# Loading k and q of the first eight attention units with consecutive rows per partition, and transposing them head by head as matmuls

## The chip, the cores and the metric

The kernel runs on one core of one Trainium2 chip. The metric is the device time of one execution in microseconds (us), and the median of three executions is compared. The engines are called as in the profile: PE (TensorE, with PEld for its weight loads), DVE (VectorE), ACT (ScalarE), POOL (GpSimd) and SP (SyncE, which issues nearly all DMA transfers; SPq is its queue).

## The reference

Attention over q, k and v of shape [4 batches, 8 heads, 576 positions, 64], then two feed-forward stages. The attention is the sum of a coarse part (q, k and v averaged over groups of four positions, a softmax over 144 keys, the result repeated four times) and a local part (each query sees the keys at a distance below 4).

```
q_d, k_d, v_d = (t.reshape(B, H, Sd, 4, D).mean(axis=3) for t in (q, k, v))
out_up = np.repeat(sm_attn(q_d, k_d, v_d), 4, axis=2)
mask = np.abs(pos[:, None] - pos[None, :]) < 4
scores = np.where(mask, scale * np.matmul(q, k.transpose(0, 1, 3, 2)), -1e9)
out_local = np.matmul(softmax(scores), v)
x = (out_up + out_local) as [2304 tokens, 512]
x = (silu(x @ w_gate) * (x @ w_val)) @ w_out              # 512 -> 1536 -> 512
h = x @ w_in
y = (np.maximum(h, 0) + alpha * np.minimum(h, 0)) @ w2_out # 512 -> 2048 -> 512
```

The weights arrive as float64, so their transfers are twice as large as float32 ones, and each is taken apart on the chip into a high and a low float32r part.

## The kernel before, in words

The attention is cut into 32 units. Unit n is two heads (hp = n mod 4) of one half of 288 queries of one batch; units 0 to 3 are the first half of batch 0 and load all of k (576 rows) and q, units 4 to 7 are its second half and load q alone, since they reuse k of units 0 to 3. These eight (NPRO = 8) run ahead of the feed-forward work, in buffers that weights will take later; units 8 to 31 are strewn into the first feed-forward stage and load k and q in another way (lines 198 to 209), which the change leaves alone.

In a unit, a_load (line 194) issues the transfers of k and q, a_T (line 288) transposes both through PSUM and copies them into kT and qT, with one column for each position, and sums groups of four columns into kd and qd; a_QK makes the local scores in 24 small matmuls per head and the coarse ones in one, and reads columns of qT and kT in the order of positions; a_EXP and a_NRM are the softmax; a_vd sums v over groups of four (line 344, DVE); a_PT and a_PV transpose the coarse weights, multiply with v and write the result as xh and xl, the inputs of the feed-forward stage.

The transfers all go through SP in an order written out by hand in the key `lo='asvtwb01x23'`: a is k and q of units 0 to 3, s and t copy v into overlapping windows in DRAM (line 260 and 266), v loads v for the sums (line 227), w loads the windows back for units 0 to 3 (line 249), b is q of units 4 to 7, the digits are the weights of feed-forward columns j = 0 to 3 (lines 104 and 106), and x loads the windows of units 4 to 7. Each k load takes one head: `k[b, h0 + h].rearrange("(r p) c -> p r c", p=QB)`, so partition p (of QB = 96) gets rows p, p + 96, p + 192 and so on, each a run of 64 floats or 256 bytes in DRAM. q is loaded in the same way, 3 rows per partition. A transpose of such a block of 96 rows and two heads (128 columns) yields 96 consecutive positions, so that the copies out of PSUM (lines 310 to 312 and 319) write consecutive columns.

The splitting of weights is prep1 and w_split (lines 509 and 124): ACT lines 129, 137 and 142, DVE line 139, and POOL or DVE line 143. A planner lays out the order of the instructions of each engine by a simulated timeline; `tc.issue_after` holds the weight work of j = 0 and 1 behind the softmax of unit 3 (gates, key 8), and the sums of line 344 behind the scores of unit 3 on DVE (line 719). From the first matmul of line 488 on, PE works through 96 feed-forward blocks of stage one and then stage two.

Of the kernel before, what the change touches and what calls it, by code (L numbers as in the profile page):

```python
# [23 lines left out]
def attn_moe_moe2_kernel(  # L24
# [13 lines left out]
    nc = tc.nc  # L38
    B, H, S, D = q.shape
# [129 lines left out]
    def at_(n, shape, tag):  # L169
        return wp.tile(shape, F32, tag=pslot[tag, n], name=tag)  # L170
# [23 lines left out]
    def a_load(n):  # L194
        b, half, hp, blk = coords(n)
        h0, t0 = 2 * hp, half * HB
        d = hu[n] = {}
        if n >= NPRO:

            loads = [("qn", q, HB, t0)]  # L200
            if half == 0:
                loads.insert(0, ("kn", k, S, 0))
            for tag, src, rn, r0 in loads:
                t = d[tag] = ap_.tile([128, rn], F32, tag=tag, name=tag, bufs=1)
                for i in range(4):
                    nc.sync.dma_start(
                        out=t[32 * i:32 * (i + 1)].rearrange("r (m c) -> r m c", c=32),
                        in_=src[b, h0 + i // 2, r0:r0 + rn, 32 * (i % 2):32 * (i % 2 + 1)].rearrange("(m r) c -> r m c", r=32))
            return
        if half == 0:  # L210
            kn = d["kn"] = at_(n, [QB, 6, 2, D], "kn")
            for h in range(2):
                nc.sync.dma_start(out=kn[:, :, h], in_=k[b, h0 + h].rearrange("(r p) c -> p r c", p=QB))
        t = at_(n, [128, 2 * NW * 2 * D], "qv").rearrange("p (a w h c) -> p a w h c", a=2, w=NW, h=2)
        d["vw"] = t[:, 1]
        qn = d["qn"] = t[:QB, 0]
        for h in range(2):
            nc.sync.dma_start(out=qn[:, :, h], in_=q[b, h0 + h, t0:t0 + HB, :].rearrange("(r p) c -> p r c", p=QB))

    def a_load_v(n):  # L220
        b, half, hp, blk = coords(n)
# [30 lines left out]
    def stage(b, halves=(0, 1)):  # L252
# [32 lines left out]
        else:  # L285
            win(g0, g1)

    def a_T(n, A):
        b, half, hp, blk = coords(n)
        d = hu[n]  # L290
        idn = ident[:QB, :QB]
        small(n)
        qT, qd = d["qT"], d["qd"]
        nc.gpsimd.memset(qT[:, HB:HB + 8], 0.0)  # L294
        if half == 0:
            kT = kTs[hp] = ap_.tile([128, KW], F32, tag=f"kT{hp}", name="kT", bufs=1)
            nc.gpsimd.memset(kT[:, 0:3], 0.0)
            nc.gpsimd.memset(kT[:, S + 3:KW], 0.0)
            kd = kds[hp] = ap_.tile([128, SD], F32, tag=f"kd{hp}", name="kd", bufs=1)
        if n >= NPRO:  # L300
            if half == 0:
                nc.vector.transpose(out=kT[:, 3:S + 3], in_=d["kn"])
            nc.vector.transpose(out=qT[:, 0:HB], in_=d["qn"])
        elif half == 0:
            for r in range(6):
                nc.tensor.transpose(A[:, r // 3, (r % 3) * QB:(r % 3 + 1) * QB], d["kn"][:, r].rearrange("p h c -> p (h c)"), idn)
            for r in range(NW):
                dst = A[:, 1, HB + QB * r:HB + QB * (r + 1)] if r < 2 else A[:, 0, 320:320 + QB]
                nc.tensor.transpose(dst, d["qn"][:, r].rearrange("p h c -> p (h c)"), idn)
            nc.scalar.copy(out=qT[:, 0:2 * QB], in_=A[:, 1, HB:HB + 2 * QB])  # L310
            nc.scalar.copy(out=qT[:, 2 * QB:HB], in_=A[:, 0, 320:320 + QB])
            nc.scalar.copy(out=kT[:, 3:S + 3].rearrange("c (f t) -> c f t", f=2), in_=A[:, :, 0:HB])
        else:
            for r in range(NW):
                nc.tensor.transpose(A[:, 0, QB * r:QB * (r + 1)], d["qn"][:, r].rearrange("p h c -> p (h c)"), idn)
            if K["qtA"]:
                nc.scalar.copy(out=qT[:, 0:HB], in_=A[:, 0, 0:HB])
            else:
                nc.vector.tensor_copy(qT[:, 0:HB], A[:, 0, 0:HB])
        if half == 0:  # L320
            if 0 < n < NP:
                kq = kT[:, 3:S + 3].rearrange("c (g r) -> c g r", r=4)
                k2 = d["sm"][:, :, 0:SD].rearrange("c h g -> c g h")
                nc.gpsimd.tensor_tensor(out=k2, in0=kq[:, :, 0:2], in1=kq[:, :, 2:4], op=ALU.add)
                nc.gpsimd.tensor_tensor(out=kd, in0=k2[:, :, 0], in1=k2[:, :, 1], op=ALU.add)
            else:
                nc.vector.reduce_sum(kd, kT[:, 3:S + 3].rearrange("c (g r) -> c g r", r=4), axis=AX.X)
        if 0 < n < NP:
            kq = qT[:, 0:HB].rearrange("c (g r) -> c g r", r=4)
            k2 = d["sm"][:, 1, 0:2 * QD].rearrange("c (g h) -> c g h", h=2)  # L330
            nc.gpsimd.tensor_tensor(out=k2, in0=kq[:, :, 0:2], in1=kq[:, :, 2:4], op=ALU.add)
            nc.gpsimd.tensor_tensor(out=qd, in0=k2[:, :, 0], in1=k2[:, :, 1], op=ALU.add)
        else:
            nc.vector.reduce_sum(qd, qT[:, 0:HB].rearrange("c (g r) -> c g r", r=4), axis=AX.X)
# [537 lines left out]
```

## Time and profile before

| | before |
|---|---|
| median of 3 runs | 1009.46 us (1009.44 to 1010.22) |
| span of the profiled execution | 1008.6 us |
| busy: PE, DVE, ACT, POOL | 970.5, 479.7, 307.6, 380.0 us |
| DMA packets, bytes | 135888, 77.80 MB |
| of them under 512 bytes | 97401 |
| k loads of units 0 to 3 | 8 of 144 KB |
| q loads of units 0 to 7 | 16 of 72 KB |

The profiled execution's own time is its span, 1008.6 us from the first to the last instruction; the 0.9 us to the median lie around it. PE is busy for 96% of the span, so the parts of the span in which it isn't are what a change outside the matmuls can reach. The page shows them at the start: in the first two of its 40 slices PE is at 5 and 6 tenths, and DMA at 7 to 9 tenths in the first four. Times in the tables are in us from the start of the span; the granted clock is 1.00 at TensorE's full 2.4 GHz and 0.50 at 1.2 GHz.

### The profile page before, as it was taken

How to read it: one execution, taken by the hardware profiler on the slowest of the kernel's cores; microseconds unless marked ns; L12 is line 12 of the kernel's file. 1: busy time of each engine (PE TensorE's matmuls, PEld its weight loads, DVE VectorE, ACT ScalarE, POOL GpSimd, SP SyncE). 2: the span in 40 equal slices, each digit the busy share in tenths (PEclk: the TensorE clock that was granted, in tenths of full speed). 3: DMA queues.
4: the chain of work that ended last, by engine and by line, in shares of the span. 5: the costliest groups of instructions: out<-in, count | busy, mean ns of one | idle time of the engine just before them, and what ended most of it. 6: DMA issues, size and time to landing. Idle time of an engine off the chain costs nothing.

```text
span 1008.6 us, 19231 instructions
## 1 busy us (share of the span) xinstructions
PE 970.5 (96%) x7760; PEld 866.4 (86%) x7760; DVE 479.7 (48%) x1010; ACT 307.6 (30%) x699; POOL 380.0 (38%) x488
## 2 busy tenths in 40 slices
PE   5689899999999999999999999999999999999998
PEld 4488799999999999999999997888888888888897
DVE  5886874464535464545432769623222222322232
ACT  4598632222222222222223656312111111211111
POOL 6487852244322334222223436624223222322222
PEclk9799999999999999999999999999999999999999
DMA  7899731132111221111104883102000100100010
GB/s 185 254 337 340 174 89 35 27 82 56 41 38 33 70 45 41 44 23 21 41 9 141 287 255 106 32 1 79 6 0 21 53 1 1 47 7 0 1 43 21
DMA packets 135888, 77.80 MB, mean 77 GB/s; under 512 B 97401, under 2 KB 127097, under 8 KB 135033
## 3 DMA queue, kind: packets, MB, share of 16 engines
q1 hardware_dynamic: 135735, 76.57, 26.9%
q8 instruction: 60, 0.98, 0.4%
q14 instruction: 29, 0.24, 0.1%
q10 hardware_dynamic: 64, 0.01, 0.0%
HBM read 67.12 MB, written 15.73 MB: 82 GB/s over the span
## 4 chain that ended last, share of the span: by engine, by line
PE 81%; DMA 7%; DVE 4%; SPq 3%; POOL 2%; ACT 2%; issue 1%; POOLq 0%; DVEq 0%; ACTq 0%
PE y L625 7%; PE y L627 7%; PE y L626 7%; PE g L488 6%; PE v L489 6%; PE v L488 6%; PE g L489 6%; PE g L490 6%; PE v L490 5%; PE y L488 4%; PE y L490 4%; PE y L489 4%; PE h L488 3%; PE h L490 3%; PE h L489 3%; DMA raw<-in_moe_w_out_dram 3%
## 5 line engine op out<-in xcount | busy, mean ns | idle before, releaser
L613 POOL TENSOR_TENSOR gl<-t,gh 128x512 fp32r<-128x512 f32 (+1 forms) x80 | 97.1, 1214 | 250.6 <-ACT gh L612 244.3
L612 ACT CAST gh<-t 128x512 fp32r<-128x512 f32 (+1 forms) x80 | 46.1, 578 | 278.5 <-DVE t L609 238.8
L488 PE MATMUL g<-xh,w 128*128 128x288 f32 x384 | 117.7, 306 | 10.4 <-DVE u L528 5.4
L490 PE MATMUL g<-xh,w 128*128 128x288 f32 x384 | 115.0, 300 | 0.8 <-POOL qT L294 0.8
L488 PE MATMUL v<-xh,w 128*128 128x288 f32 x384 | 115.7, 301 | 0.1
L489 PE MATMUL v<-xl,w 128*128 128x288 f32 x384 | 115.1, 300 | 0.0
L489 PE MATMUL g<-xl,w 128*128 128x288 f32 x384 | 114.8, 299 | 0.0
L489 PE MATMUL y<-pl,w 128*128 128x288 f32 x384 | 113.9, 299 | 0.8 <-POOL pl L538 0.8
L625 PE MATMUL y<-w,gh 128*128 128x512 f32 x288 | 113.2, 393 | 1.0 <-ACT sy L557 1.0
L490 PE MATMUL v<-xh,w 128*128 128x288 f32 x384 | 113.3, 295 | 0.0
L490 PE MATMUL y<-ph,w 128*128 128x288 f32 x384 | 113.0, 297 | 0.0
L626 PE MATMUL y<-w,gh 128*128 128x512 f32 x288 | 112.8, 392 | 0.0
L627 PE MATMUL y<-w,gl 128*128 128x512 f32 x288 | 112.0, 392 | 0.0
L528 DVE SCALAR_TENSOR_TENSOR u<-u,g 128x288 f32<-128x288 f32 x96 | 43.3, 451 | 143.0 <-ACT u L527 142.9
L488 PE MATMUL y<-ph,w 128*128 128x288 f32 x384 | 110.9, 302 | 0.0
L538 POOL TENSOR_TENSOR pl<-u,ph 128x288 fp32r<-128x288 f32 x96 | 81.6, 850 | 56.9 <-ACT ph L537 56.5
L143 POOL TENSOR_TENSOR w<-st,w 128x512 fp32r<-128x512 f32 x52 | 70.7, 1366 | 55.6 <-ACT w L142 55.3
L488 PEld LDWEIGHTS g<-xh,w 128*128 128x128 f32 x384 | 73.3, 191 | 14.2 <-DVE u L528 7.4
L607 DVE TENSOR_SCALAR t<-h,alpha 128x512 f32<-128x512 f32 (+1 forms) x40 | 27.9, 696 | 110.7 <-PE h L490 109.5
L488 PEld LDWEIGHTS y<-ph,w 128*128 128x128 f32 x384 | 70.8, 189 | 4.5 <-issue 4.4
L490 PEld LDWEIGHTS g<-xh,w 128*128 128x128 f32 x384 | 73.6, 192 | 1.1 <-POOL qT L294 1.1
L527 ACT ACTIVATE u<-g 128x288 f32<-128x288 f32 x96 | 39.3, 409 | 115.4 <-PE g L490 109.3
(197 smaller groups left out, 2148.2 us busy)
## 6 DMA issues: line engine op xcount, KB each, us to landing
raw<-in_moe_w_out_dram SPq DMA_DIRECT2D x28, 512.0 KB
raw<-in_moe_w_in_dram SPq DMA_DIRECT2D x16, 512.0 KB
raw<-in_moe_w_gate_dram SPq DMA_DIRECT2D x12, 512.0 KB
raw<-in_moe_w_val_dram SPq DMA_DIRECT2D x12, 512.0 KB
vw<-vwin SPq DMA_DIRECT2D x48, 96.0 KB
out_dram<-os SPq DMA_DIRECT2D x18, 256.0 KB
sy<-y SPq DMA_DIRECT2D x16, 256.0 KB
y<-ys SPq DMA_DIRECT2D x14, 288.0 KB
```

The costliest lines, as they stand in the source:

```text
L143: eng.tensor_sub(w[:, 1], st, f32(w[:, 0]))
L488: nc.tensor.matmul(o, lhi, rhi, start=first, stop=False)
L489: nc.tensor.matmul(o, lhi, rlo, start=False, stop=False)
L490: nc.tensor.matmul(o, llo, rhi, start=False, stop=last)
L527: nc.scalar.activation(out=u, in_=GV[0][:, :HB], func=AF.Tanh, scale=0.5)
L528: nc.vector.scalar_tensor_tensor(out=u, in0=u, scalar=1.0, in1=GV[0][:, :HB], op0=ALU.add, op1=ALU.mult)
L538: nc.gpsimd.tensor_sub(pl, u, f32(ph))
L612: nc.scalar.copy(out=gh[:, :n], in_=t[:, :n])
L613: nc.gpsimd.tensor_sub(gl[:, :n], t[:, :n], f32(gh[:, :n]))
L625: nc.tensor.matmul(o, gh[:, ms], ohi, start=(j == 0), stop=False)
L626: nc.tensor.matmul(o, gh[:, ms], olo, start=False, stop=False)
L627: nc.tensor.matmul(o, gl[:, ms], ohi, start=False, stop=(j == F2 - 1))
```

## The change

For units 0 to 7, one transfer loads both heads of k, and one both heads of q. A partition gets consecutive rows: 6 of k per head (a run of 1536 bytes in DRAM) and 3 of q (768 bytes). In SBUF a tile then lies by head, row and channel. Since the two heads of one row are no longer side by side, the new helper two_T makes each transpose from two matmuls with the identity as the moving operand, one per head, into the lower and the upper 64 partitions of PSUM. A transposed block now holds every sixth (k) or every third (q) position, so the copies out of PSUM put the columns back in order: they write with a step of 6 or 3 floats. Everything behind kT and qT is as before.

```diff
@@ -208,14 +208,14 @@
                         in_=src[b, h0 + i // 2, r0:r0 + rn, 32 * (i % 2):32 * (i % 2 + 1)].rearrange("(m r) c -> r m c", r=32))
             return
         if half == 0:
-            kn = d["kn"] = at_(n, [QB, 6, 2, D], "kn")
-            for h in range(2):
-                nc.sync.dma_start(out=kn[:, :, h], in_=k[b, h0 + h].rearrange("(r p) c -> p r c", p=QB))
+            kn = d["kn"] = at_(n, [QB, 2, 6, D], "kn")
+            nc.sync.dma_start(out=kn.rearrange("p h r c -> p h (r c)"),
+                              in_=k[b, h0:h0 + 2].rearrange("h (p r) c -> p h (r c)", p=QB))
         t = at_(n, [128, 2 * NW * 2 * D], "qv").rearrange("p (a w h c) -> p a w h c", a=2, w=NW, h=2)
         d["vw"] = t[:, 1]
-        qn = d["qn"] = t[:QB, 0]
-        for h in range(2):
-            nc.sync.dma_start(out=qn[:, :, h], in_=q[b, h0 + h, t0:t0 + HB, :].rearrange("(r p) c -> p r c", p=QB))
+        qn = d["qn"] = t[:QB, 0].rearrange("p w h c -> p (w h c)").rearrange("p (h r c) -> p h r c", h=2, r=NW)
+        nc.sync.dma_start(out=qn.rearrange("p h r c -> p h (r c)"),
+                          in_=q[b, h0:h0 + 2, t0:t0 + HB, :].rearrange("h (p r) c -> p h (r c)", p=QB))
 
     def a_load_v(n):
         b, half, hp, blk = coords(n)
@@ -285,12 +285,17 @@
         else:
             win(g0, g1)
 
+    def two_T(dst, src, idn):
+        for h in range(2):
+            nc.tensor.matmul(dst[64 * h:64 * h + 64], src[:, h], idn, start=True, stop=True)
+
     def a_T(n, A):
         b, half, hp, blk = coords(n)
         d = hu[n]
         idn = ident[:QB, :QB]
         small(n)
         qT, qd = d["qT"], d["qd"]
+        qR = qT[:, 0:HB].rearrange("c (p r) -> c r p", r=NW)
         nc.gpsimd.memset(qT[:, HB:HB + 8], 0.0)
         if half == 0:
             kT = kTs[hp] = ap_.tile([128, KW], F32, tag=f"kT{hp}", name="kT", bufs=1)
@@ -303,20 +308,21 @@
             nc.vector.transpose(out=qT[:, 0:HB], in_=d["qn"])
         elif half == 0:
             for r in range(6):
-                nc.tensor.transpose(A[:, r // 3, (r % 3) * QB:(r % 3 + 1) * QB], d["kn"][:, r].rearrange("p h c -> p (h c)"), idn)
+                two_T(A[:, r // 3, (r % 3) * QB:(r % 3 + 1) * QB], d["kn"][:, :, r], idn)
             for r in range(NW):
                 dst = A[:, 1, HB + QB * r:HB + QB * (r + 1)] if r < 2 else A[:, 0, 320:320 + QB]
-                nc.tensor.transpose(dst, d["qn"][:, r].rearrange("p h c -> p (h c)"), idn)
-            nc.scalar.copy(out=qT[:, 0:2 * QB], in_=A[:, 1, HB:HB + 2 * QB])
-            nc.scalar.copy(out=qT[:, 2 * QB:HB], in_=A[:, 0, 320:320 + QB])
-            nc.scalar.copy(out=kT[:, 3:S + 3].rearrange("c (f t) -> c f t", f=2), in_=A[:, :, 0:HB])
+                two_T(dst, d["qn"][:, :, r], idn)
+            nc.scalar.copy(out=qR[:, 0:2], in_=A[:, 1, HB:HB + 2 * QB].rearrange("c (r p) -> c r p", r=2))
+            nc.scalar.copy(out=qR[:, 2], in_=A[:, 0, 320:320 + QB])
+            nc.scalar.copy(out=kT[:, 3:S + 3].rearrange("c (p f r) -> c f r p", f=2, r=NW),
+                           in_=A[:, :, 0:HB].rearrange("c f (r p) -> c f r p", r=NW))
         else:
             for r in range(NW):
-                nc.tensor.transpose(A[:, 0, QB * r:QB * (r + 1)], d["qn"][:, r].rearrange("p h c -> p (h c)"), idn)
+                two_T(A[:, 0, QB * r:QB * (r + 1)], d["qn"][:, :, r], idn)
             if K["qtA"]:
-                nc.scalar.copy(out=qT[:, 0:HB], in_=A[:, 0, 0:HB])
+                nc.scalar.copy(out=qR, in_=A[:, 0, 0:HB].rearrange("c (r p) -> c r p", r=NW))
             else:
-                nc.vector.tensor_copy(qT[:, 0:HB], A[:, 0, 0:HB])
+                nc.vector.tensor_copy(qR, A[:, 0, 0:HB].rearrange("c (r p) -> c r p", r=NW))
         if half == 0:
             if 0 < n < NP:
                 kq = kT[:, 3:S + 3].rearrange("c (g r) -> c g r", r=4)
```

## Rows read from the trace of the kernel before

**Rows 1.** Busy time by stage: us, engines (instructions), granted clock, DMA share, GB/s

```profile
0.00:36.00 36.00, 22.06 (x326) 16.77 (x326) 22.76 (x61) 14.58 (x49) 19.34 (x59) 1.00 0.71 183
36.00:59.00 23.00, 13.75 (x232) 11.02 (x232) 19.22 (x46) 21.28 (x52) 16.08 (x21) 0.70 1.04 327
59.00:75.00 16.00, 16.00 (x179) 15.01 (x180) 12.49 (x27) 14.66 (x40) 14.37 (x16) 0.90 0.91 328
75.00:97.00 22.00, 20.83 (x163) 19.39 (x161) 15.17 (x25) 18.25 (x39) 17.27 (x16) 1.00 1.06 372
97.00:135.00 38.00, 32.27 (x313) 29.30 (x314) 33.39 (x64) 23.97 (x48) 30.75 (x32) 0.96 0.68 157
```

**Rows 2.** Chain that ended last, in order of time: start, us, what

```profile
20.08 9.09 DMA qv<-vwin
...
33.66 5.85 DMA raw<-in_moe_w_out_dram
...
58.94 0.61 PE g L488
...
60.27 0.24 PE g L489
...
63.44 0.13 PE v L488
```

**Rows 3.** SP's queue in order of time: start, us, line, transfer, count

```profile
0.74 0.94 SPq L213 DMA_DIRECT2D kn<-in_k_dram  x2
...
8.07 1.03 SPq L218 DMA_DIRECT2D qv<-in_q_dram  x2
...
29.59 2.97 SPq L218 DMA_DIRECT2D qv<-in_q_dram  x6
...
32.60 0.47 SPq L106 DMA_DIRECT2D raw<-in_moe_w_gate_dram  x1
```

**Rows 4.** DMA in steps of 2 us: us, clock, DMA share, GB/s

```profile
4.00:6.00 2.00, 1.00 0.98 215
6.00:8.00 2.00, 1.00 1.05 215
...
36.00:38.00 2.00, 1.00 1.08 385
```

**Rows 5.** PE in order of time: start, us from first start to last end

```profile
6.76 1.19 PE L306 MATMUL y<-ident,kn 96*128 96x96 f32 x6 [0.71 <-DMA kn<-in_k_dram]
...
15.10 0.42 PE L309 MATMUL gv<-ident,qv 96*128 96x96 f32 x1
...
41.73 1.17 PE L465 MATMUL gv<-bd,qv 128*64 128x96 f32 x12
...
43.90 0.74 PE L315 MATMUL y<-ident,qv 96*128 96x96 f32 x3
```

**Rows 6.** POOL in order of time, units 1 to 3

```profile
7.44 1.30 POOL L676 COPY mask<-tmp 32x128 f32<-32x128 f32 x4
...
19.80 0.31 POOL L332 TENSOR_TENSOR qs<-qs 128x72 f32<-128x72 f32 x1
```

**Rows 7.** Who waited for whom up to 40 us: total us, times, longest

```profile
POOL qs L386 <- DVE mx L373: 2.9, 2, 1.8
```

**Rows 8.** DVE in order of time, from the scores of unit 3

```profile
21.83 0.32 DVE L369 TENSOR_TENSOR qs<-gv,mask 128x192 f32<-128x192 f32 x1
...
24.30 7.76 DVE L344 TENSOR_REDUCE vs<-vd 72x128 f32<-72x512 f32 x8
...
37.66 0.69 DVE L139 SCALAR_TENSOR_TENSOR st<-st 128x512 int32<-128x512 int32 x1 [0.76 <-ACT st L137]
```

**Rows 9.** Groups by shape, first 60 us: busy us, mean ns of one

```profile
L344 DVE TENSOR_REDUCE vs<-vd 72x128 f32<-72x512 f32 x8 | 7.8, 1036 | 0.0
...
L370 DVE TENSOR_REDUCE mx<-y 72x2 f32<-72x288 f32 x4 | 1.8, 444 | 0.0
...
L312 ACT COPY kT<-y 128x576 f32<-128x576 f32 x2 | 1.3, 664 | 0.0
```

## The prediction, made before the changed kernel ran

> **What bounds the kernel now.** I read the stages first. Up to 36 us PE is busy for 22.1 of 36 us, and much of that is short matmuls that wait for one another; from 59 to 75 us it is busy throughout; between 97 and 135 us it has 5.7 us of idle time once more [rows 1]. What runs before 59 us is therefore a lead-in that PE cannot shorten, and whatever moves the first lasting feed-forward matmul (line 488 at 58.94 us) moves the end, if the weights behind it move as well.
>
> The chain of waits says what the lead-in is made of: the transfers of the windows, then the first weight (w_out) landing, each as long as 9.09 and 5.85 us, and then ACT, POOL and DVE steps up to the matmul [rows 2]. So I read SP's queue. Units 0 to 3 cost it sixteen issues, from 0.74 us to the end of the last at 9.10 us, a pitch of (9.10 - 0.74) / 16 = 0.52 us; the eight q loads of units 4 to 7 stand before the weights, six of them in 2.97 us, 0.50 us each; the first weight is issued at 32.60 us [rows 3]. DMA is at the limit at the same time: 215 GB/s at a share of 0.98 to 1.05 while the 256-byte runs of k and q are under way, against 385 GB/s at 1.08 when weights with runs of 1 KB and more follow [rows 4].
>
> Last I read the engines. After the mask is copied (end 8.74 us) POOL makes kd and qd of units 1 to 3 up to 20.11 us [rows 6], and in between it waits 2.9 us for DVE, twice [rows 7]. DVE takes up unit 3's scores at 21.83 us, then spends 7.76 us on the sums of v, and is at the first weight (line 139) at 37.66 us, having idled 0.76 us [rows 8]. From 36 to 59 us ACT is busy for 21.3 of 23 us and DVE for 19.2 [rows 1]: there the engines bound the lead-in.
>
> **The transfers of units 0 to 3.** Sixteen issues become eight. I keep 0.52 us for one, since the first weight's issue, of 512 KB, takes 0.47 us [rows 3] and bytes thus hardly count; the ends are 0.47 and 0.94 us (the two it replaces). The stage transfers then start 8 x 0.52 = 4.2 us earlier (at worst 0, at best 4.6). The bytes stay: 4 x (295 + 147) KB = 1.77 MB. At 215 GB/s they take 8.2 us, at 385 GB/s 4.6 us, so DMA gives back 3.6 us. The runs of 768 and 1536 bytes have no row of their own; I take the weights' rate as the nearer, with 215 GB/s (no gain) as the other end. Issue and data agree on about 4 us for unit 3's k and q; unit 0's wait for the first bytes hardly shrinks.
>
> **The transfers of units 4 to 7.** Eight issues become four, 4 x 0.50 = 2.0 us, and 0.59 MB go from 2.7 to 1.5 us. They stand ahead of the weights, so the first weight can be issued up to 4.2 + 2.0 = 6.2 us earlier, near 26.4 us. No wait is added; a transfer of two heads lands as one, so that a unit's first transpose waits for both heads, as it does now, since each block holds both.
>
> **The transposes.** 36 for units 0 to 3 and 12 for units 4 to 7 become 96 matmuls of half the width. Now, six take 1.19 us; taking off the tail of one (about 0.37 us), the pitch is 0.82 / 5 = 0.16 us. The same shape as the new ones exists: line 465 is a plain matmul of 64 stationary and 96 moving columns into alternating halves of PSUM, twelve in 1.17 us, a pitch of (1.17 - 0.37) / 11 = 0.073 us. Line 315's three transposes right after it, in the same low-clock stretch, take 0.74 us, a pitch of 0.18 [rows 5]. A pair thus costs 0.15 where a transpose costs 0.16 to 0.18: nothing, and I count nothing (ends: -0.02 and +0.16 us for a pair, the latter if two halves don't overlap; nine pairs of a unit then cost 1.4 us). In units 0 to 3 the ACT and POOL chains cover them; without that cover they would add the 1.4 us for each of three units.
>
> A page speaks against this. The Trainium skill ("TensorE: Matmul & The Clock Gate", Terms) says that transpose mode is 4x faster for float32; by it the new matmuls would be four times as dear as what they replace. Line 465's rows disagree with it for this shape [rows 5]; it stays as a rival below.
>
> **The copies out of PSUM.** They write with a step of 12 bytes (q) or 24 (k). No row shows a strided write on ACT or DVE. The nearest is a strided read: line 344 reads with a step of 256 bytes and takes 1036 ns for 512 elements; line 370 reads 288 in a row in 444 ns, and at that pace, 1.54 ns each, 512 would take 789 ns [rows 9]. That is 31% more. On line 312 (664 ns [rows 9]) it is 0.2 us, with lines 310 and 311 0.35 us for a unit. I take +0.4 us on the path in all: two DVE copies of line 319 (0.14 us each) stand directly ahead of line 139, and one ACT copy ends the load of unit 3. The bounds are 0 and a doubling, which is 1.2 us for each of units 0 to 3.
>
> The Trainium skill ("SBUF — State Buffer", Door 1) says that an access which crosses to a new 16-byte line each time pays a penalty; k's step of 24 bytes does, q's of 12 mostly does. It gives no figure, so the sum stays by line 344.
>
> **What of it reaches the end.** The 4 us of arrival are not all taken up. Unit 0 is hardly earlier, the mask stays at 8.74 us, and POOL then has 11.37 us up to 20.11, of which it waits 2.9 us [rows 6, 7]. Earlier k and q can remove that wait and little more. I take 2.6 us of the 2.9, since unit 1's k, which PE waits 0.71 us for [rows 5], no longer holds the chain. DVE's scores of unit 3 go from 21.83 to about 19.2 us, and with them the sums of v and all up to line 139. The 0.76 us of idle there is a wait for the first weight, which comes 6 us earlier: it goes. The sum is 2.6 + 0.76 - 0.4 = 3.0 us at line 139. From 36 to 97 us DMA is at a share of 0.91 to 1.06 [rows 1]; the weight stream starts earlier by more than 3 us, so it does not hold this back, and the 5.7 us of later idle hang on the same conversions, moved by the same amount. What is late next is ACT and DVE between 36 and 59 us.
>
> By the profiled execution, a span of 1008.6 becomes 1005.6 us; with the 0.9 us around it, and so beside the median of 1009.46, I predict **1006.5 us**. Its own range, by the bounds of arrival (2.0 to 3.1 us) and of the copies (0 to 1.2 us), is 1005 to 1008 us.
>
> **The rivals.**
> - *More passes.* The planner uses the weights that come 6.2 us earlier to fill the ACT time left before 36 us (14.6 of 36 us busy [rows 1]), so that the crowded stretch behind it thins out as well. The full 6.2 us: 1003.3 us. Against it: the weight work is held behind unit 3's softmax. Chance 0.17.
> - *It is hidden.* ACT and DVE are full from 36 to 59 us; if the work there is what sets line 488, and the planner fills the time in front with nothing, only the 0.76 us go: 1008.7 us. Chance 0.22.
> - *Slower: PE overtakes.* The planner lays out a new order, and PE's blocks come ahead of the conversions they need. The clock falls when PE idles: it is 0.70 from 36 to 59 us, and at half clock a feed-forward matmul takes 0.24 us where it takes 0.13 later [rows 1, 2]. A block of 24 matmuls at half clock costs 24 x 0.11 = 2.6 us. Two such blocks and the gain lost give 1009.5 + 5.2 = 1014.7 us, one gives 1012.1. It decides from the point at which PE's idle time between 97 and 135 us grows by more than the 3.0 us gained. Chance 0.13, about 1012.
> - *The transposes are dear.* At four times the pitch, nine blocks cost 9 x 0.49 = 4.4 us more in a unit, which no longer fits between its copies; 3 units behind one another cost 13 us less 3 us: 1020 us. Chance 0.03.
> - *It doesn't do what it says.* If runs of 768 bytes and more moved no faster than 256, the eight larger transfers would still be bound by 8.2 us of data; what is left is the 2.0 us of issues that stand ahead of the weights and 0.76 us at line 139 at best: 1008.7 to 1009.5 us. Chance 0.05, with the hidden case for sign.
>
> **How the numbers follow.** The forecast has 0.40. A measurement of this kernel can tell about 0.2%, 2.0 us, from no change. Faster by more: the forecast nearly whole (0.38) and the first rival (0.17), with a few of the hidden case, 0.58 in all. Within: the rest of the hidden case, the case of no faster transfer and the edge of the forecast, 0.26. Slower: the two dear cases, 0.16. For 8 in 10 the range runs from 1002.5, which takes in most of the first rival, to 1011.5 us, which leaves out most of those two.
>
> **What would show it.** Right: the k and q loads of units 0 to 3 end on SP's queue near 4.9 us and the first weight is issued near 27 us; the DMA rate in 2 to 6 us is above 300 GB/s; packets fall by about 6900 (9216 of 256 bytes against 768 and 1536); POOL's two waits are shorter; DVE takes up unit 3's scores near 19 us and line 488 begins near 56 us; a pair of new matmuls keeps the pitch of 0.15 us. Wrong: line 488 still near 59 us with the transfers early (hidden); the copies at more than 1.3 times their durations; a granted clock below 0.96 between 97 and 135 us with more idle time there (PE overtakes).

## The result and the profile after

The changed kernel takes 1023.48 us (median of 4 runs, 1022.08 to 1024.77) where the kernel before takes 1009.45: a ratio of 1.0133, 95% interval 1.0120 to 1.0147, or 14.0 us more, where 3 us less was forecast. Its profiled execution took 1024.4 us, with a span of 1022.3 us against 1008.6.

The transfers did what the change says. SP's queue of the kernel after, answering [rows 3] (start, us, line, transfer, count):

```profile
5.18 0.45 SPq L217 DMA_DIRECT2D qv<-in_q_dram  x1
5.67 0.96 SPq L260 DMA_DIRECT2D vwin<-in_v_dram  x1
...
25.32 0.92 SPq L217 DMA_DIRECT2D qv<-in_q_dram  x2
26.30 1.22 SPq L106 DMA_DIRECT2D raw<-in_moe_w_gate_dram  x1
```

Eight issues end at 5.63 us, and the first weight is issued at 26.30 us instead of 32.60. The page's count of packets, against 135888 and 97401 before:

```profile
DMA packets 128785, 77.82 MB, mean 76 GB/s; under 512 B 87993, under 2 KB 119993, under 8 KB 127929
```

The rate rose little. The same 2-us windows as in [rows 4], of after (the last two figures are DMA's share and GB/s):

```profile
4.00:6.00 2.00, 1.70 (x22) 1.73 (x24) 0.00 (x0) 0.00 (x0) 2.00 (x10) 1.00 0.83 213
6.00:8.00 2.00, 2.00 (x29) 2.00 (x28) 0.00 (x0) 0.51 (x3) 1.88 (x13) 1.00 1.10 249
```

PE shows what the transposes became. PE of after in order of time, answering [rows 5]:

```profile
4.30 2.19 PE L290 MATMUL att<-ident,kn 96*64 96x96 f32 x24 [4.30 <-DMA kn<-in_k_dram]
6.25 1.20 PE L290 MATMUL att<-ident,qv 96*64 96x96 f32 x12
...
14.68 0.76 PE L366 MATMUL y<-kT,qs 64*32 64x32 f32 x48
16.47 0.76 PE L370 MATMUL y<-kd,qs 64*72 64x144 f32 x4 [1.03 <-POOL qs L338]
17.16 0.42 PE L290 MATMUL y<-ident,qv 96*64 96x96 f32 x1
```

A k is 12 matmuls, since it has six blocks and a pair for each, yet the row counts 24 records: a plain float32 matmul leaves two records, a transpose one (and so does a feed-forward matmul, in float32r). The local scores show it too: line 366 makes 24 matmuls for a unit, 12 for each of its two heads and not 24, in 48 records. The block takes 2.19 us where six transposes took 1.19 [rows 5], a q takes 1.20 instead of some 0.7. The last rows show an order that before did not have: the last matmul of unit 2's q (17.16) stands behind unit 1's coarse scores (16.47, line 370), which wait 1.03 us for POOL. ACT of after shows the same kind of order, and the copies with a step:

```profile
7.49 0.41 ACT L315 COPY qs<-att 128x192 f32<-128x192 f32 x1 [4.63 <-PE att L290]
7.75 0.29 ACT L316 COPY qs<-att 128x96 f32<-128x96 f32 x1
7.88 1.20 ACT L317 COPY kT<-att 128x576 f32<-128x576 f32 x1
...
16.41 0.72 ACT L433 ACTIVATE qs<-qs,sr 72x144 f32<-72x144 f32 x2 [0.93 <-DVE sr L422]
17.78 0.42 ACT L315 COPY qs<-y 128x192 f32<-128x192 f32 x1 [0.65 <-PE y L290]
```

Line 317 takes 1.20 us where line 312 took 0.66 [rows 9]. Unit 2's copies (17.78) stand behind the softmax scaling of unit 0 (line 433). So the units run one behind another, and DVE gets to unit 3's scores, and to the first weight, later than in [rows 8]. DVE of after:

```profile
29.89 0.36 DVE L375 TENSOR_TENSOR qs<-gv,mask 128x192 f32<-128x192 f32 x1
...
30.98 7.78 DVE L350 TENSOR_REDUCE vs<-vd 72x128 f32<-72x512 f32 x8
...
42.77 0.69 DVE L139 SCALAR_TENSOR_TENSOR st<-st 128x512 int32<-128x512 int32 x1
...
79.44 0.34 DVE L375 TENSOR_TENSOR qs<-att,mask 128x192 f32<-128x192 f32 x1
```

Unit 3's scores come 8.1 us later than before (21.83), line 139 comes 5.1 us later (37.66), and unit 7's scores, the last row, come at 79.44 us where before they come at 69.30. The stages, answering [rows 1] in the same windows:

```profile
0.00:36.00 36.00, 23.57 (x402) 19.64 (x404) 18.06 (x50) 15.35 (x44) 17.07 (x54) 1.00 0.78 228
36.00:59.00 23.00, 16.29 (x234) 13.16 (x230) 18.95 (x40) 17.59 (x43) 14.50 (x20) 1.00 1.02 309
59.00:75.00 16.00, 11.88 (x124) 10.41 (x125) 13.06 (x29) 13.92 (x37) 10.59 (x14) 0.79 1.06 378
75.00:97.00 22.00, 19.98 (x203) 18.30 (x203) 19.46 (x34) 19.59 (x45) 18.69 (x18) 0.90 0.68 218
97.00:135.00 38.00, 32.21 (x254) 30.15 (x254) 33.74 (x51) 25.62 (x52) 32.33 (x32) 0.93 0.69 178
```

From 59 to 75 us PE was busy throughout before; now it idles 4.1 us, and the granted clock is 0.79, 0.90 and 0.93 in the last three windows where it was 0.90, 1.00 and 0.96. What PE waits for from 48 to 135 us:

```profile
PE g L494 <- DVE u L534: 6.9, 3, 3.6
PE g L494 <- DVE qs L476: 3.7, 1, 3.7
PE att L467 <- ACT qs L450: 1.2, 1, 1.2
```

The lag of after against before can be followed along the feed-forward matmuls of the two timelines: the first begins at 53.68 us against 47.66 (6.0 us late), the 25th at 66.94 against 58.94 (8.0), the 169th at 99.57 against 85.88 (13.7), the 1001st at 240.31 against 226.54 (13.8), and there it stays. Of the 13.8 us, 6.0 are there when feed-forward begins, and nearly all of the remaining 7.8 arise within 50 us. Where they lie is told by each kernel's own stretch from its first feed-forward matmul to its 1001st, before first, then after:

```profile
47.66:226.54 178.88, 168.61 (x1711) 157.12 (x1712) 121.03 (x266) 91.06 (x215) 106.07 (x132) 0.97 0.55 158
53.68:240.31 186.63, 171.73 (x1721) 160.57 (x1722) 126.10 (x265) 90.87 (x212) 103.35 (x130) 0.95 0.48 134
```

PE idles 14.9 us in after's stretch and 10.3 in before's, 4.6 us more, and it is busy 3.1 us longer with the same feed-forward matmuls. Some 2.3 of these 3.1 us are speed: two feed-forward matmuls in a row begin 0.24 us apart 105 times in after and 84 times in before, and 0.13 us apart nearly everywhere else, so 21 more cost 0.11 us each. But for rounding, 6.0 + 4.6 + 3.1 us make the 13.8: the lag is a late start, more waiting, and more matmuls at the lower speed.

### The profile page after: what moved, and what is told of

The parts are those of the page before. It is cut to its first block, busy times and chain, and to the rows that moved or that the text cites. A ratio compares the mean times of both kernels' runs of the same rounds, so it can differ in the third digit from the quotient of the medians.

```text
span 1022.3 us, 19498 instructions
## 1 busy us (share of the span) xinstructions
PE 982.0 (96%) x7904; PEld 877.7 (86%) x7904; DVE 485.9 (48%) x1010; ACT 310.3 (30%) x699; POOL 379.0 (37%) x488
## 4 chain that ended last, share of the span: by engine, by line
PE 83%; DVE 6%; DMA 4%; ACT 3%; POOL 2%; issue 1%; SPq 0%; DVEq 0%; POOLq 0%; ACTq 0%
PE y L631 6%; PE y L633 6%; PE y L632 6%; PE g L494 6%; PE v L495 6%; PE v L494 6%; PE g L495 6%; PE g L496 6%; PE v L496 6%; PE y L494 4%; PE y L496 4%; PE y L495 4%; PE h L494 3%; PE h L496 3%; PE h L495 3%; DMA raw<-in_moe_w_in_dram 2%
## 5 line engine op out<-in xcount | busy, mean ns | idle before, releaser
L544 POOL TENSOR_TENSOR pl<-u,ph 128x288 fp32r<-128x288 f32 x96 | 79.4, 828 | 59.4 <-ACT ph L543 59.0
L494 PEld LDWEIGHTS g<-xh,w 128*128 128x128 f32 x384 | 73.3, 191 | 14.7 <-DVE u L534 9.5
L495 PEld LDWEIGHTS y<-pl,w 128*128 128x128 f32 x384 | 73.1, 190 | 4.2 <-POOL pl L544 3.5
```

The costliest lines, as they stand in the source:

```text
L494: nc.tensor.matmul(o, lhi, rhi, start=first, stop=False)
L495: nc.tensor.matmul(o, lhi, rlo, start=False, stop=False)
L544: nc.gpsimd.tensor_sub(pl, u, f32(ph))
```

## The experiments

Three theories were put forward: **P**, the loss is the time that the new matmuls and strided copies themselves take; **S**, the copies or the loads are the cause; **O**, the planner lays out units 0 to 3 in another order, and the order costs. Theories **E** and **L**, **D** and **U** came later and concern units 4 to 7.

### The parts, one by one

**l_only**: the loads alone, single transposes over two rows of one head.

```diff
+            kn = d["kn"] = at_(n, [QB, 2, 6, D], "kn")
+            nc.sync.dma_start(out=kn.rearrange("p h r c -> p h (r c)"), in_=k[b, h0:h0 + 2].rearrange("h (p r) c -> p h (r c)", p=QB))
-                nc.tensor.transpose(A[...], d["kn"][:, r].rearrange("p h c -> p (h c)"), idn)
+                nc.tensor.transpose(A[...], d["kn"].rearrange("p h r c -> p (h r c)")[:, 128 * r:128 * r + 128], idn)
```

> The changed kernel with its loads, but each block transposed as one transpose of 128 neighbouring columns and copied without a step (heads and positions come out mixed up, so the attention of units 0 to 7 is not computed rightly; shapes and sizes are those of before). Theory O and P: what the prediction worked out for the loads, with nothing against it: 3 to 4 us less than before, 1005.5 to 1006.5 us, unit 3's scores near 19 us. If the earlier loads are worth nothing, or shift the order of the weights for the worse: 1009 to 1012 us.

Measured: 1010.14 us, ratio 0.9998 (0.9983 to 1.0013). The first weight is issued at 26.87 us, 5.7 us earlier than before, and nothing of it arrives at the end. PE of l_only in order of time shows why the front gains nothing:

```profile
4.15 1.19 PE L289 MATMUL att<-ident,kn 96*128 96x96 f32 x6 [4.15 <-DMA kn<-in_k_dram]
...
7.68 1.22 PE L289 MATMUL y<-ident,kn 96*128 96x96 f32 x6 [1.86 <-DMA kn<-in_k_dram]
```

Unit 0's k is there no earlier, and unit 1's is first used 0.9 us later than in [rows 5] (6.76), although it is issued at 1.66 us where before issues it at 2.78. In both kernels unit 0's k and q stand ahead of it on the queue. That it now shares DMA with more transfers, since all eight are issued by 5.7 us, is possible; no run singled that out.

**s_only**: the strided copies, with the old loads in the new row order (`(r p)` becomes `(p r)`), so that the result stays right.

```diff
-            nc.scalar.copy(out=kT[:, 3:S + 3].rearrange("c (f t) -> c f t", f=2), in_=A[:, :, 0:HB])
+            nc.scalar.copy(out=kT[:, 3:S + 3].rearrange("c (p f r) -> c f r p", f=2, r=NW), in_=A[:, :, 0:HB].rearrange("c f (r p) -> c f r p", r=NW))
```

> The kernel before with transposes and one transfer for each head, but consecutive rows per partition and so the copies out of PSUM with a step of 3 or 6 floats. The copy of k takes 1.20 us with the step where it takes 0.66 without, and that of q 0.71 in two where it takes 0.56. Theory S: 1016 us or more. Theories O and P: 0.7 us for a unit on ACT, of which one to three units lie on the path: 1009.5 to 1012 us.

Measured: 1016.82 us, 1.0068 (1.0047 to 1.0090). This kernel mixes two things: its loads are slower than either kernel's (window of s_only, last figure GB/s; before has 215 there):

```profile
4.00:6.00 2.00, 1.01 (x7) 1.04 (x8) 0.00 (x0) 0.00 (x0) 2.00 (x10) 1.00 0.69 156
```

**l_and_s**: both edits together, with single transposes, so that the copies stand on the new loads.

> The changed kernel with one transpose of 128 neighbouring columns in place of the two matmuls (the attention of units 0 to 7 is not computed rightly; shapes and sizes are as in the changed kernel); the copies keep their step. Against l_only, which lacks the step, it tells the price of the strided copies alone: the planned order of PE is the same in both. By the trace of the changed kernel the step costs 0.69 us on ACT for each of units 0 to 3 and 0.1 us on DVE for the others. Where that lies on the path once to three times: 1010.5 to 1013 us. If the 7 us of s_only came from the step and not from its slower loads: 1016 us or more.

Measured: 1010.18 us, 1.0004 (0.9994 to 1.0015). The step of the copies costs nothing measurable at the end, so theory S falls for the changed kernel. What s_only lost is then more likely due to its slower loads; no run has these loads without the step.

**t_only** and **t_again**: the pairs of matmuls alone, on the old loads.

```diff
+    def two_T(dst, src, idn):
+        for h in range(2):
+            nc.tensor.matmul(dst[64 * h:64 * h + 64], src[:, h], idn, start=True, stop=True)
-                nc.tensor.transpose(dst, d["qn"][:, r].rearrange("p h c -> p (h c)"), idn)
+                two_T(dst, d["qn"][:, r], idn)
```

> The kernel before, with its own loads and copies, and only each transpose of units 0 to 7 made from two matmuls with the identity, one per head. In the trace of the changed kernel the twelve matmuls for one k have 24 records and take 2.19 us, where six transposes take 1.19; the planned order of PE puts the last matmul of a unit's q behind the coarse scores of the unit before. Theory O (the matmuls make the planner lay out an order in which each of units 0 to 3 waits for the one before, and that is most of the 14 us): 1016 to 1024 us, unit 3's scores on DVE at 27 us or later. Theory P (only the prices of matmuls and copies add up, order is no matter): 1.46 us more on PE for each of four units at most, 1011 to 1015 us, unit 3's scores at 23 to 26 us. Theory S (the strided copies or the loads are the cause): 1009 to 1010 us.

> The kernel of t_only once more, for a second trace: its executions lay at 1015 us once and at 1022 to 1025 three times, and the trace was of the 1015. If the difference is TensorE's clock: a trace of a longer execution shows more time at 1.2 GHz between 60 and 130 us than the 13.6 us of the first, and the same times up to 50 us.

Measured: 1022.95 us, 1.0114 (1.0075 to 1.0154), and 1019.72 us, 1.0102 (1.0071 to 1.0132). t_only's trace is of its shortest execution, 1015.36 us; the other three took 1022.37 to 1024.87. Against it t_again's (1019.19 us) is the same to 0.3 us up to 50 us, and from 60 to 130 us PE idles 3.3 us more, at a granted clock of 0.88 and not 0.91: waiting makes the difference as well as the clock. **l_and_t** joins them with the loads of l_only:

> The changed kernel with copies without a step (the positions of q and k come out in another order, so that the local attention of units 0 to 7 is not computed rightly). The two matmuls and the loads stay. Theory O: the order of PE is that of the changed kernel, and nearly all of the loss stays, 1016 to 1024 us. If the step is what the loss needs beside the order: 1010 to 1014 us.

Measured: 1021.84 us, 1.0128 (1.0102 to 1.0154). The pairs of matmuls carry the loss, whatever they are joined with.

### Order or price

**order_locked**: the kernel before, single transposes, with the last q transpose of units 1 to 3 held behind the coarse scores of the unit before, as after has it on PE.

```diff
+                    if 0 < n < NP and r == NW - 1:
+                        es.enter_context(tc.issue_after(lastqk[n - 1]))
```

> The kernel before with one edit: the last transpose of q of units 1 to 3 is held behind the coarse scores of the unit before, as the planner does by itself where the transposes are matmuls. Loads, transposes and copies are those of before. Theory O (the order costs, since a unit's copies then start only when the unit before has made its scores): unit 3's scores on DVE at 25 to 27 us in place of 21.8, and 1013 to 1018 us. Theory P (the price of matmuls and copies costs): at most 1 us at the scores, 1009 to 1011 us.

Measured: 1019.12 us, 1.0091 (1.0067 to 1.0115), with no work added. **before_reordered** takes over after's order on ACT and DVE as well:

```diff
+            with ExitStack() as es:
+                if n < NP and n - 2 in scl:
+                    es.enter_context(tc.issue_after(scl[n - 2]))
                 nc.scalar.copy(out=qT[:, 0:2 * QB], ...)
+            if n < NP and n - 1 in bdl:
+                es.enter_context(tc.issue_after(bdl[n - 1]))
             nc.vector.tensor_tensor(out=sm[:, :, 0:LW], in0=A[:, :, 0:LW], in1=mk, op=ALU.add)
```

> The kernel before, with its own loads, transposes and copies, but units 0 to 3 in the order of after: on PE the last transpose of a q behind the coarse scores of the unit before, on ACT a unit's copies behind the scaling of the unit two before, on DVE its scores behind the block transposes of the unit before. Theory O: nearly the whole loss at no price at all, ratio 1.009 to 1.013 (order_locked, with PE alone, gave 1.009), unit 3's scores at 25 to 27 us. Theory P: at most 1.004.

Measured: 1017.56 us, 1.0076 (1.0059 to 1.0093). Order without price thus costs 8 to 9 us. But taking the new order away does not give the loss back in full. **order_fixed** puts all transposes of units 0 to 3 ahead of all scores in after:

```diff
         for n in range(NP):
             a_T(n, P[n])
+        for n in range(NP):
             a_QK(n, P[n])
             gate(n, 0)
```

> The changed kernel with one edit: the transposes and copies of units 0 to 3 are written ahead of all their scores, so that the planner puts the 72 matmuls of these units first on PE. Prices stay as in the changed kernel. Theory O: at least half of the 14 us come back, 1009 to 1016 us, unit 3's scores near 24 us or earlier. Theory P: at most 2 us come back, 1021 to 1024 us.

Measured: 1017.66 us, 1.0078 (1.0055 to 1.0102): by the ratios, some 5.5 of the 13.4 us come back, which lies between the two theories. **before_first** is the control for it, the kernel before with the scores of units 0 to 3 held behind unit 3's last transpose:

```diff
+                    with ExitStack() as es:
+                        if n < NP:
+                            es.enter_context(tc.issue_after(lastT[0]))
                         nc.tensor.matmul(A[SWIN * i:SWIN * (i + 1), h, w * SWIN:(w + 1) * SWIN], ...)
```

> The kernel before, with the transposes of units 0 to 3 all ahead of the scores of units 0 to 3 in PE's planned order, that is the PE order of order_fixed up to the second weights' blocks, but with the single transposes, loads and copies of before. Theory O (the planned order alone makes the loss): as slow as order_fixed, ratio near 1.008 (1006 to 1010 per mille), unit 0's scores near 14.5 us as there. Theory P (the order of order_fixed is harmless and the 8 us left there are the price of the two matmuls and of the copies): within 0.2% of before. Between: what before_first lacks to order_fixed is the price at a fixed order; from the extra records (1.0 us a k, 0.46 us a q, 0.7 us a unit of copies) I put that at 2 to 4 us, so a ratio of 1.004 to 1.006.

Measured: 1013.93 us, 1.0040 (1.0027 to 1.0053). order_fixed stands 1.0078 - 1.0040 above its control, 3.8 us, within some 1 to 6.5. That is no price at one order yet: on PE the two traces agree up to unit 3's scores, near 18 us, and differ behind them (unit 7's last products stand behind 158 feed-forward matmuls in order_fixed and 180 in before_first), and the loads are not the same.

**after_ahead** and **before_ahead** write each unit's transposes one unit ahead of the scores, in after and in before.

```diff
+        a_T(0, P[0])
         for n in range(NP):
-            a_T(n, P[n])
+            if n + 1 < NP:
+                a_T(n + 1, P[n + 1])
             a_QK(n, P[n])
```

> The kernel after, written so that each unit's transposes stand one unit ahead of the scores: in PE's planned order all six matmuls of a unit's q are then ahead of the coarse scores of the unit before, where in after the sixth was behind them. Prices of matmuls, copies and loads unchanged. Theory O: most of the 14 us is returned; unit 3's scores near 23 to 25 us (after 29.9), ratio 1.001 to 1.005 (1010.5 to 1014.5 us). Theory P: 1018 to 1024 us, as after. If only some 6 us come back as in order_fixed (1016 to 1018), the extra matmul time itself carries the rest.

> The same rewriting on the kernel before, the control for after_ahead. In before no matmul of a q stands behind coarse scores of an earlier unit but unit 1's and unit 3's third, so theory O expects little: 0.996 to 1.002, unit 3's scores 20 to 22 us. What after_ahead stands above this run is the price of the change at nearly one order: theory O 1 to 4 us, theory P 10 to 14 us.

Measured: 1022.31 us, 1.0125 (1.0109 to 1.0142), and 1013.93 us, 1.0040 (1.0025 to 1.0055). So after_ahead stands 8.6 us above its control (some 6 to 11), between what theory O (1 to 4) and theory P (10 to 14) gave for that. These two don't share their order in full either: unit 6's last products stand behind 96 feed-forward matmuls in after_ahead and 57 in before_ahead. The price of the change beside a control written alike is thus 3.8 us once and 8.6 us once, and no pair of runs has it by itself. In after_ahead PE's order of units 0 to 3 was put right, yet ACT still had the copies of unit 2 behind unit 0's scaling, and the units still ran one behind another. **after_ordered** and **ordered_again** (one kernel, run twice) therefore give after the order of before on PE, ACT and DVE:

```diff
+        for w, n in (("T", 0), ("T", 1), ("Q", 0), ("T", 2), ("T", 3), ("Q", 1), ("Q", 2), ("Q", 3)):
+            with aft(n, kc.get(3) if n == 1 else None):
                 a_EXP(n)
+            with aft(n, kc.get(2) if n == 0 else None, pq.get((n + 2, 1 + n)) if n < 2 else None, sc.get(2) if n == 1 else None):
                 a_NRM(n)
```

(`aft` holds what follows behind the named copy kc, POOL sum pq or DVE step sc of another unit.)

> The kernel after, with loads, pairs of matmuls and strided copies unchanged, but units 0 to 3 in the order of before: on PE the transposes of units 2 and 3 ahead of the scores of unit 1, on ACT the copies of unit 2 ahead of unit 0's scaling and those of unit 3 ahead of unit 1's exponentials, on DVE unit 2's scores ahead of unit 1's sums. Theory O (the order on all engines is the loss): unit 3's scores at 23 to 25 us, ratio 1.000 to 1.004 (1009.5 to 1013.5 us), little above before. Theory P (the time of the matmuls and copies is the loss): 1.009 to 1.013, whatever the order. Between these, both carry a part, in that proportion.

> after_ordered once more, for its trace. If units 0 to 3 do run in the order of before there, unit 3's scores stand at 23 to 26 us and the first feed-forward matmul at 49 to 52 us, and the rest of its loss (13 us in all) comes behind that, between 55 and 130 us; if not, the scores stand near 28 us and the first feed-forward matmul near 54 us, as in after.

Measured: 1022.38 us (three executions; a fourth is told of at the end), 1.0127 (1.0110 to 1.0144), and 1020.93 us, 1.0107 (1.0083 to 1.0131). In the second trace unit 3's scores are back at 23.02 us and the first feed-forward matmul at 48.51 us, 0.9 us behind before, and still the 1001st is 10.6 us late. Between these two PE idles 18.5 us, where before idles 10.3. Theory O in its first form, that the order of units 0 to 3 is the loss, falls with this run: the late start can be taken away, and the loss comes back behind it. PE's waits of ordered_again from 48 to 135 us:

```profile
PE g L505 <- DVE u L545: 8.6, 3, 6.3
PE y L505 <- ACT ph L554: 3.8, 1, 3.8
PE y L458 <- ACT qs L444: 3.7, 1, 3.7
```

### Which units

**t_first** has the pairs in units 0 to 3 alone, **t_last** in units 4 to 7 alone, where t_last's one edit is

```diff
         else:
             for r in range(NW):
-                nc.tensor.transpose(A[:, 0, QB * r:QB * (r + 1)], d["qn"][:, r].rearrange("p h c -> p (h c)"), idn)
+                two_T(A[:, 0, QB * r:QB * (r + 1)], d["qn"][:, r], idn)
```

and t_first has t_only's others.

> The kernel before with the pair of matmuls in units 0 to 3 alone (k and q), single transposes in units 4 to 7. On PE units 0 to 3 stand in the order of t_only; unit 7's last product stands behind 108 feed-forward matmuls (60 in before, 79 in t_only). Theory E (the loss is made in units 0 to 3): first feed-forward matmul near 51 us as in t_only (before 47.7), ratio 1.008 to 1.012. Theory L (it is made by units 4 to 7 among the first feed-forward blocks): 1.003 or less, unless unit 7's new place costs by itself.

> The kernel before with the pair of matmuls in units 4 to 7 alone (q, three pairs a unit, 1.4 us of PE more in all). PE's order of units 0 to 3 is that of before; unit 7's last product stands behind 96 feed-forward matmuls as in after (60 in before). Theory E: first feed-forward matmul near 48 us, ratio 0.998 to 1.002. Theory L: 1.005 to 1.009, the part of the loss that after shows behind its first feed-forward matmul.

Measured: 1020.68 us, 1.0107 (1.0085 to 1.0130), and 1017.12 us, 1.0074 (1.0056 to 1.0091). Each half carries most of a loss of its own, and both together (t_only) are no worse than the first: it is no sum of prices. t_last is the sharper case. Units 0 to 3 run as in before (unit 3's scores at 21.58 us), and 12 transposes become 24 matmuls, at 0.166 us more for a pair some 2 us; it loses 7.5. Its planned order differs from before on DVE behind unit 3's block transposes (before on the left; lines 323 and 338 are before's 319 and 334):

```
before                                     t_last
L319 COPY qs<-att        (unit 4's q)      L139 first weight
L319 COPY qs<-y          (unit 5's q)      L323 COPY qs<-att        (unit 4's q)
L139 first weight                          L139 second weight
L334 sum of unit 4's q                     L338 sum of unit 4's q
L139 second weight                         L323 COPY qs<-y          (unit 5's q)
```

and on PE, where unit 6's last products stand behind 96 feed-forward matmuls (before: 60; it is unit 6 that the expectations above call unit 7). After has both orders too. **t_last_copies** undoes the first, **t_last_unit7** the second:

```diff
+        for n in (NP, NP + 1):
+            a_T(n, P[n - NP])
+        with tc.issue_after(qcp[NP + 1]):
             preps(K["pre"][1])
```

```diff
+            if ffn[0] == 21:
+                for i in early:      # unit 7's coarse scores, unit 6's last product
+                    es.enter_context(tc.issue_after(i))
             nc.tensor.matmul(o, lhi, rhi, start=first, stop=False)
```

> t_last, with the q copies of units 4 and 5 ahead of the first weight conversion on DVE, as in before; on PE the last units stay late (unit 7's coarse scores behind 84 feed-forward matmuls, unit 6's last products behind 101). Theory D (the place of the copies on DVE makes the loss): first feed-forward matmul back near 48 us (t_last 50.2), ratio 1.000 to 1.003. Theory U (the place of units 6 and 7 among the feed-forward blocks makes it): 1.006 to 1.010, as t_last or more.

> t_last, with unit 7's coarse scores and unit 6's last products made to stand ahead of the 21st triple of feed-forward matmuls as written: on PE behind 60 and 72 of them (before 60 and 60, t_last 60 and 96). The copies on DVE stay behind the weight conversions. Theory U: 1.000 to 1.003, unit 7's scores near 71 us (t_last 74.2). Theory D: 1.006 to 1.009, as t_last, with the first feed-forward matmul near 50 us.

Measured: 1020.63 us, 1.0111 (1.0095 to 1.0126), and 1016.46 us, 1.0071 (1.0054 to 1.0087). The first does bring the first feed-forward matmul to 45.76 us, 1.9 us ahead of before, and loses more; the second leaves unit 7's scores at 74.81 us. Neither theory holds by itself.

### All of them side by side

Each row is one profiled execution (us from the start of the span): DVE's scores of unit 3 and of unit 7, and the start of the first and the 1001st feed-forward matmul. (t_only's is the shortest of its four executions.)

| kernel | unit 3 | first ff | unit 7 | 1001st ff |
|---|---|---|---|---|
| before | 21.83 | 47.66 | 69.30 | 226.54 |
| l_only | 22.36 | 49.63 | 71.80 | 227.93 |
| l_and_s | 22.47 | 49.81 | 72.42 | 228.11 |
| before_ahead | 21.65 | 47.20 | 70.64 | 229.02 |
| before_first | 22.25 | 49.98 | 72.26 | 229.19 |
| t_only | 27.15 | 50.94 | 75.13 | 230.66 |
| t_last | 21.58 | 50.19 | 74.15 | 232.40 |
| s_only | 23.05 | 51.44 | 74.19 | 233.28 |
| before_reordered | 26.11 | 48.17 | 77.24 | 234.05 |
| t_last_unit7 | 22.12 | 49.80 | 74.81 | 234.46 |
| order_fixed | 24.73 | 51.92 | 75.14 | 234.63 |
| t_last_copies | 21.77 | 45.76 | 75.07 | 234.84 |
| t_again | 27.37 | 51.16 | 75.78 | 235.14 |
| order_locked | 25.83 | 47.99 | 77.00 | 235.46 |
| t_first | 27.76 | 49.55 | 74.44 | 236.54 |
| after_ahead | 28.46 | 53.82 | 77.40 | 236.93 |
| ordered_again | 23.02 | 48.51 | 77.18 | 237.12 |
| after | 29.89 | 53.68 | 79.44 | 240.31 |
| l_and_t | 28.27 | 52.12 | 78.65 | 242.08 |

Over these 19 executions the 1001st matmul goes with unit 7's scores (correlation 0.91), less with unit 3's (0.69) and least with the first feed-forward matmul (0.44). For the 25th, the one at 58.94 us on which the prediction had rested, it is 0.65. That unit 7's lateness is the cause is not shown: no run moved it alone. It may as well be a mark of how far ACT, DVE and POOL have come with units 4 to 7 and the weights, which they share. What stays open is which place in the new order sets it. No version came out ahead of the kernel before; l_only and l_and_s equal it.

## Why the prediction was wrong, point by point

- **SP's issues: right.** 5.63 us for the last of eight (4.9 forecast, at a pitch of 0.61 us, not 0.52), 26.30 us for the first weight (26.4 forecast), 7103 packets fewer (some 6900 forecast).
- **DMA at the weights' rate: wrong.** 213 and 249 GB/s, with 300 named as the sign of being right and 385 reckoned with; the other end that was named, 215, was nearly it. Of the 3.6 us of data little is left, and the first k is no earlier.
- **The transposes cost nothing: the step that failed.** Line 465's row x12 was taken for twelve matmuls. The loop in a_PV makes six, two heads by three windows, so the pitch of a matmul is twice what was read, and of the two ends given for a pair the upper one (+0.16 us, 1.4 us a unit) was what came: 24 records in 2.19 us, less the tail of 0.37, are (2.19 - 0.37) / 11 = 0.165 us a call, 0.33 a pair, against 0.164 for a transpose. The pairs carry the whole loss: without them the kernel is as fast as before (l_only, l_and_s), with them alone it loses 10 to 12 us (t_only, t_again). "ACT and POOL chains cover them" failed with it, since these chains follow the transposes. The price by itself is still too small: all 48 pairs add 48 x 0.166 = 8.0 us to PE at most, and 14.0 us were lost.
- **The copies +0.4 us: wrong as to size, right at the end.** 1.20 against 0.66 us is 1.8 times, near the doubling that was the upper bound; l_and_s shows that it costs nothing measurable at the end.
- **2.6 us of POOL's wait, 0.76 us at line 139: wrong.** Even with the loads alone unit 3's scores come at 22.36 us, not 19.2, and line 139 at 38.06 us, 0.4 us later than before, though its wait of 0.76 us is gone there. l_only's 1010.14 us lies near the rivals *It is hidden* (1008.7 us) and *It doesn't do what it says* (1008.7 to 1009.5). The first fits in the time alone, since unit 3's scores gained nothing that the work from 36 to 59 us could have hidden; the second is nearer to what the rows show.
- **The rival *PE overtakes* came nearest to the mechanism** (a new planned order, PE idle, half clock) and had a chance of 0.13 and a price of 2.6 us for one block. Its place was wrong: from 97 to 135 us PE idles no more than before (38 - 32.21 against 38 - 32.27 us), though the clock there is 0.93; the idle time grew from 59 to 97 us. Its price was short, because it left out the late start of 6.0 us and took the replanning for one or two blocks, where order_locked, with no work added, lost 9.2 us.
- **The rival *The transposes are dear*** gave 1020 us, near the result, by luck. It took a pair to cost four times a transpose, and the rows do not bear that out. The Trainium skill ("TensorE: Matmul & The Clock Gate", Terms) has transpose mode as 4 times faster for float32; here a pair takes twice a transpose's time.

The forecast also took the order of all other work as given, and priced only work that is moved and added; a new order stood in it as a rival alone. How much of the loss is price and how much is order stays open. Four of the kernels above (order_locked, before_reordered, before_first, before_ahead) change nothing but the order, and lose 4 to 9 us.

## What to carry to other kernels

Where a planner orders the queues, an added or dearer instruction also costs what it does to the whole order, and kernels that add no work at all show how far that can reach: here 4 to 9 us, as much as the 3.8 and 8.6 us that two changed kernels took beyond controls written alike. Before a pitch is taken from a row's count, hold the count against the loops of the code. And a gain or loss at one milestone, such as the first feed-forward matmul, says little until the work that shares its engines behind it has been followed as well.

## What the runs showed of the hardware

Plain float32 matmuls leave two records in the trace and transposes one. The granted clock of the rows reads 1.00 from the start, yet in order_fixed the pitch of the pairs nearly halves while PE works without a gap. Windows of order_fixed, PE alone (busy us, records, granted clock, DMA):

```profile
7.00:10.00 3.00, 3.00 (x42) 1.00 1.02 276
10.00:13.00 3.00, 3.00 (x72) 1.00 0.79 294
```

and two blocks of k in the same kernel:

```profile
7.10 2.16 PE L290 MATMUL y<-ident,kn 96*64 96x96 f32 x24
...
11.72 1.17 PE L290 MATMUL gv<-ident,kn 96*64 96x96 f32 x24
```

The same 24 records take 2.16 and 1.17 us at a granted clock of 1.00 both times, a ratio of 1.85 and so near that of the two levels. The feed-forward matmuls of after tell the same: from 53.68 to 57.93 us they begin 0.24 us apart, in a window whose granted clock reads 1.00, and from 60.98 us 0.13 us apart. So the granted clock of these rows is no guide to TensorE's speed in the lead-in, and the price of a pair there is that of the lower speed. Later it is less: a q takes 1.20 us at 6.14 us in order_fixed, and 0.67 us at 68.05 us in t_last.

Runs of 768 and 1536 bytes moved at 213 to 249 GB/s, where 256-byte runs had 215 and weights 385 [rows 4]. In s_only, where a transfer of one head takes the new row order, so that its rows follow one another in DRAM but land 512 bytes apart in SBUF, the rate fell to 145 to 185 GB/s from 2 to 10 us.

One execution of after_ordered took 5245.8 us, at a granted clock of 1.00 throughout; a feed-forward matmul took 1.15 us in it, where ordered_again has 0.31, while DVE was busy for 476.7 us, about as long as in before (479.7), so that only PE was slow:

```profile
L505 PE MATMUL g<-xh,w 128*128 128x288 f32 x384 | 440.8, 1148 | 0.0
```

The kernel's other five ran at 1021 to 1023 us. What this was is not explained; its trace is used for nothing here.
